# The second MLP matmul of a retention-and-MLP kernel: the plain product in every block in place of a seven-product form

## The chip, the cores and the metric

The kernel runs on one core of one Trainium2 chip. The metric is the time of one execution in microseconds (us). A "slow" or "fast" label stands beside each execution; slow means more than 1.5% above the fastest execution of the same kernel in the same rounds. The profile names the engines PE (TensorE matmul), PEld (TensorE weight load), DVE (VectorE), ACT (ScalarE), POOL (GpSimd) and SP.

## The reference

```python
def _attn_ref(q, k, v):                      # (8, 8, 576, 64) each
    scores = (1 / np.sqrt(64)) * q @ k.transpose(0, 1, 3, 2)
    ret = scores * Dmat                      # decay gamma ** (i - j), causal
    return ret @ v

def _moe_ref(x, w_in, w_out):                # x (4608, 512), w_in (512, 2048), w_out (2048, 512)
    h = x @ w_in
    g = h * np.cos(h)                        # the "gated units" of the middle layer
    return g @ w_out                         # the second MLP matmul
```

The kernel handles the 4608 tokens in nine blocks of 512. A block's second matmul multiplies 512 x 2048 gated units by 2048 x 512 second weights.

## The kernel before

Every operation is a task in a graph. A list scheduler in Python gives each task a planned length and fixes, once and for all, the order of instructions on every engine. Two forms of the second matmul exist. `plain2` is the ordinary product. `wino2` splits the units, the tokens and the output columns of a block in two and uses seven products in place of eight, at the price of sums of operands. The sums of second weights are made once (`wsums`), the sums of gated units in each block. The kernel before uses `plain2` for block 0 alone.

```python
class Kernel:
    PLAIN = (0,)
    ...
    def plain2(self, j, base, span):            # 4 token tiles x 16 units, 512 columns each
        for half in range(2):
            for tt in range(2):
                for qd in range(4):             # 16 tasks of 4 matmuls, planned at 864 ns
                    for f in range(4 * qd, 4 * qd + 4):
                        e.matmul(bank (128 x 512), gt[f] (128 tokens), w_out[f] (512 columns), ...)
                copy("act", bank -> os)         # 4 copies on ACT a block
            self.store(j, half, os)             # 512 KB
    ...
    def wino2(self, j, base, span):
        # 8 sums of gated units of 128 x 1024 on DVE: S1, S2, S3, S4, each in two parts
        # 7 products x 8 units x 2 token tiles = 112 matmuls of 256 columns, in three banks
        # 3 snapshots and 1 copy on ACT, 3 combinations of outputs on DVE
        ...
                if j == NTB - 1:                # the last block stores its last half in two parts
                    self.store(j, 1, os[1], (256, 512))
                    self.store(j, 1, os[1], (0, 256))
    ...
    def graph(self):
        ...
        for j in range(NTB):
            if j == 1:
                self.wsums()                    # 8 sums of second weights on DVE, two of them in place
            ...                                 # first matmul (mlp1) of block j + 1
            if j in self.PLAIN:
                self.plain2(j, base, PER)
            else:
                self.wino2(j, base + 900, 12200 if last else PER)
            ...                                 # attention sessions for blocks to come
```

(Shortened and partly paraphrased in comments; cuts are marked.) The scheduler also holds a model of how blocks of instructions reach TensorE, with the constant `FETCH = 6000` ns; two experiments use it.

## Time and profile before

| | before |
|---|---|
| time, median of first runs | 308.1 us (307.5 to 313.1) |
| profiled execution | 312.0 us, labelled slow, clock 0.994 |
| PE busy | 294.1 us, 95% of the span |
| DVE busy | 206.3 us, 66% |
| last matmul to end of span | 3.2 us |

"PE busy" is a union of modelled durations, so 95% is only a hint; the prediction below shows the lines from which it takes that PE sets the time. In the lines, `L763` is the first MLP matmul, `L886` the seven-product matmul, `L800` the plain second matmul, `L774` (DVE) makes the gated units `gt`, `L847` and `L853` make the sums `s` of gated units, and `L634`, `L643`, `L652`, `L661` are the small attention matmuls, which come in sessions of 128. `pt` (`L723`, DVE) holds the decayed scores, and `xt` is the attention output that ACT's copy (`L476`) hands to the first MLP matmul.

### The profile page before, as it was taken

To read this page: it belongs to the slowest core of one execution; us is meant where nothing else is said; L and a number is where in the kernel's file an instruction comes from. 1 tells how busy PE (TensorE), PEld (TensorE's weight loads), DVE (VectorE), ACT (ScalarE), POOL (GpSimd) and SP (SyncE) were. 2 spreads that over 40 slices of the span, in tenths; PEclk is the share of its full clock that TensorE was granted. 3 is DMA by queue.
4 is the path that set the end of the run, shared out by engine and by line. 5 is a ranking of instruction groups with operands and counts; after the bars stand their busy time and mean duration, and the time that the engine had idled before them with its cause. 6 is when DMAs were issued, how large, how long until landed. Compare 5 with 4: busy or idle time off the path is not lost.

```text
span 310.3 us, 10091 instructions
## 1 busy us (share of the span) xinstructions
PE 294.1 (95%) x4274; PEld 214.7 (69%) x4277; DVE 206.3 (66%) x371; ACT 188.3 (61%) x340; POOL 108.9 (35%) x134
## 2 busy tenths in 40 slices
PE   8987999799889999999998799999999999999995
PEld 8866755688778888567855375768656666666684
DVE  3574973475984769898478487775769667666641
ACT  3476843888959775856373566474686665455430
POOL 2261058759517581931362631312741000000000
PEclk9999999999999999999999799999999999999999
DMA  9999999999977999894999749269701100300123
GB/s 172 222 159 206 205 229 217 253 270 219 219 157 189 122 204 285 159 171 109 234 219 247 181 48 235 61 114 195 161 13 72 70 2 0 127 10 2 63 76 136
DMA packets 126397, 46.80 MB, mean 151 GB/s; under 512 B 105104, under 2 KB 122000, under 8 KB 126352
## 3 DMA queue, kind: packets, MB, share of 16 engines
q1 hardware_dynamic: 122128, 41.95, 63.3%
q0 software_dynamic: 4224, 4.19, 8.4%
q8 instruction: 34, 0.56, 0.8%
q14 instruction: 11, 0.09, 0.1%
HBM read 36.70 MB, written 9.44 MB: 149 GB/s over the span
## 4 chain that ended last, share of the span: by engine, by line
PE 87%; DVE 3%; ACT 3%; issue 2%; DMA 2%; POOL 2%; DVEq 0%
PE bk L763 39%; PE bk L886 32%; PE bk L800 4%; PE bk L418 2%; DMA stgq<-in_q_dram 2%; PE bk L661 2%; PE bk L652 2%; PE bk L634 2%; PE st L643 2%; PE bk L575 2%; DVE gt L774 1%; PE bk L593 1%; DVE pt L723 1%; POOL win L743 1%; POOL wout L747 1%
## 5 line engine op out<-in xcount | busy, mean ns | idle before, releaser
L774 DVE TENSOR_TENSOR gt<-bk,cb 128x256 bf16<-128x256 f32 (+1 forms) x192 | 103.7, 555 | 59.5 <-ACT cb L771 52.9
L763 PE MATMUL bk<-xt,win 128*128 128x256 bf16 (+1 forms) x768 | 140.1, 327 | 2.3 <-issue 1.3
L771 ACT ACTIVATE cb<-bk,cpi 128x256 bf16<-128x256 f32 (+1 forms) x192 | 108.4, 585 | 55.6 <-PE bk L763 54.0
L763 PEld LDWEIGHTS bk<-xt,win 128*128 128x128 bf16 x768 | 72.9, 98 | 44.0 <-issue 2.3
L512 POOL TENSOR_TENSOR natv<-stgv,wv 128x512 bf16<-128x512 f32 x38 | 41.3, 1097 | 36.1 <-DMA stgv<-in_v_dram 23.3
L477 POOL CAST natk<-stgk 128x512 bf16<-128x512 f32 x36 | 22.0, 626 | 62.0 <-DMA stgk<-in_k_dram 34.6
L557 POOL TENSOR_TENSOR qnat<-stgq,wq 128x512 bf16<-128x512 f32 x36 | 38.6, 1092 | 13.5 <-DMA stgq<-in_q_dram 5.9
L723 DVE TENSOR_TENSOR pt<-bk,tri 128x512 bf16<-128x512 f32 (+1 forms) x46 | 29.6, 683 | 14.8 <-PE st L643 12.8
L476 ACT ACTIVATE sbd<-st 128x512 bf16<-128x512 f32 x32 | 19.3, 603 | 22.6 <-PE st L643 22.4
L886 PE MATMUL bk<-wout,s 128*128 128x256 bf16 x256 | 32.2, 273 | 0.0
L886 PE MATMUL bk<-tw,s 128*128 128x256 bf16 x256 | 31.6, 273 | 0.5 <-DVE s L847 0.5
L886 PE MATMUL bk<-wout,gt 128*128 128x256 bf16 x256 | 31.6, 273 | 0.0
L886 PEld LDWEIGHTS bk<-wout,s 128*128 128x128 bf16 x256 | 24.7, 98 | 6.6
L886 PEld LDWEIGHTS bk<-tw,s 128*128 128x128 bf16 x256 | 24.6, 98 | 6.1 <-DVE s L847 0.8
L886 PEld LDWEIGHTS bk<-wout,gt 128*128 128x128 bf16 x256 | 24.7, 98 | 4.6 <-DVE pt L723 0.2
L476 ACT ACTIVATE sn<-bk 128x512 f32<-128x512 f32 x24 | 14.4, 604 | 18.7 <-PE bk L886 18.7
L476 ACT ACTIVATE xt<-bk 128x512 bf16<-128x512 f32 x36 | 23.1, 694 | 0.3 <-PE bk L661 0.2
L898 DVE TENSOR_TENSOR os<-bk,sn 128x512 f32<-128x512 f32 x24 | 16.4, 685 | 8.2 <-PE bk L886 8.2
L886 PE MATMUL bk<-tw,gt 128*128 128x256 bf16 x128 | 17.3, 282 | 0.0
L886 PEld LDWEIGHTS bk<-tw,gt 128*128 128x128 bf16 x128 | 12.9, 101 | 4.2 <-issue 0.6
L418 PE MATMUL bk<-one 128*128 128x128 bf16 x181 | 14.3, 244 | 1.1 <-DVE lq L441 1.1
L800 PE MATMUL bk<-wout,gt 128*128 128x512 bf16 x61 | 14.8, 379 | 0.2
(63 smaller groups left out, 230.7 us busy)
## 6 DMA issues: line engine op xcount, KB each, us to landing
stgk<-in_k_dram SPq DMA_DIRECT2D x32, 256.0 KB, 5.0
stgv<-in_v_dram SPq DMA_DIRECT2D x32, 256.0 KB, 5.4
out_dram<-os SPq DMA_DIRECT2D x15, 512.0 KB, 3.5
stgq<-in_q_dram SPq DMA_DIRECT2D x12, 512.0 KB, 7.0
stgq<-in_q_dram SPq DMA_DIRECT2D x8, 256.0 KB, 4.9
win<-in_moe_w_in_dram POOLq DMA_DIRECT2D x4, 512.0 KB, 7.6
wout<-in_moe_w_out_dram POOLq DMA_DIRECT2D x4, 512.0 KB, 14.7
out_dram<-os SPq DMA_DIRECT2D x6, 256.0 KB, 3.5
```

The costliest lines, as they stand in the source:

```text
L418: inst = e.matmul(ap(self.at(self.wb), 512, 0, 128, 0, [1, 128]), self.ONE.ap(), self.ONE.ap(), start=True, stop=True, skip_group_check=True)
L476: return self.one(eng, dur, lambda e: e.activation(dst(), src(), AF.Copy), r=r, w=w, **kw)
L477: return self.one(eng, dur, lambda e: e.tensor_copy(dst(), src()), r=r, w=w, port=True, **kw)
L512: self.one(ve, vd, lambda e, b2=b2: e.tensor_tensor(ap(self.at(t["natv"]), 1024, 0, 128, 512 * b2, [D, H], [1, D]), ap(self.at(t["stgv"]), ...
L557: self.one("dve" if fast else "pool", 620 if fast else 990, lambda e, t=t, y=y: e.tensor_tensor(ap(self.at(t["qnat"]), 1024, 0, 128, y * 5 ...
L723: self.one("dve", 610, lambda e, hp=hp: e.tensor_tensor(ap(self.at(pt), 1024, p0, n, 512 * hp, [64, 8], [1, 64]), ap(self.at(sc[hp]), 512, ...
L763: inst = e.matmul(ap(self.at(bk), 512, 0, 128, 0, [1, n]), ap(self.WIN, 4 * DFF, 0, 128, c * DFF + 128 * f, [1, 128]), ap(self.at(xt), 204 ...
L771: self.one("act", 70 + n, lambda e: e.activation(ap(self.at(cb), TB, 0, 128, 0, [1, n]), ap(self.at(bk), 512, 0, 128, 0, [1, n]), AF.Sin, ...
L774: self.one("dve", 75 + n / 0.96, lambda e: e.tensor_tensor(ap(self.at(gt), NF * TB, 0, 128, f * TB + 256 * h0, [1, n]), ap(self.at(bk), 51 ...
L800: inst = e.matmul(self.at(bk).ap(), ap(self.at(gt), NF * TB, 0, 128, f * TB + 256 * half + 128 * tt, [1, 128]), ap(self.WOUT, NF * DM, 0, ...
L886: inst = e.matmul(ap(self.at(bank), 512, 0, 128, 256 * tt, [1, 256]), l(f, tt), rr(f), start=(first and f == 0 and tt == 0), stop=True, sk ...
L898: self.one("dve", 610, lambda e: e.tensor_tensor(view(h, c), ap(self.at(bank), 512, 0, 128, 0, [256, 2], [1, 256]), ap(self.at(sn[name]), ...
```

## The change

The intent is to drop the sums, at the price of a seventh more multiplications in the second matmul (eight products for seven).

```diff
-    PLAIN = (0,)
+    PLAIN = tuple(range(NTB))
...
-            if j == 1:
+            if j == 1 and len(self.PLAIN) < NTB:
                 self.wsums()
```

## The prediction

> **What bounds the kernel now.** I read the page's first two parts first, then PE's own waits, then the table by stretches, then the chain in order of time, and last the groups by line with their shapes.
>
> The head of the page and PE's rows over 40 slices:
>
> ```profile
> PE 294.1 (95%) x4274; PEld 214.7 (69%) x4277; DVE 206.3 (66%) x371; ACT 188.3 (61%) x340; POOL 108.9 (35%) x134
> ...
> PE   8987999799889999999998799999999999999995
> ...
> DVE  3574973475984769898478487775769667666641
> ...
> PEclk9999999999999999999999799999999999999999
> ```
>
> PE is busy for 95% of the span, and DVE reaches nine tenths only in a few slices between about 50 and 150 us. So PE is the first suspect. "Busy" does not prove it, because a matmul's end is modelled. The table by stretches (us from the start) says where PE is not full:
>
> ```profile
> 24.00:55.00 31.00, 29.17 (x288) 19.74 (x282) 19.63 (x38) 18.67 (x40) 11.70 (x13) 1.00 1.21 214
> 55.00:80.00 25.00, 23.18 (x451) 19.64 (x452) 15.39 (x33) 21.32 (x45) 18.84 (x22) 1.00 1.11 245
> 80.00:100.00 20.00, 18.06 (x366) 15.08 (x364) 15.35 (x30) 15.11 (x33) 9.24 (x12) 1.00 0.85 184
> 100.00:125.00 25.00, 24.90 (x566) 21.42 (x565) 18.67 (x39) 18.12 (x41) 12.75 (x15) 1.00 1.03 198
> ...
> 150.00:175.00 25.00, 21.72 (x363) 14.05 (x361) 15.02 (x22) 13.01 (x21) 11.43 (x13) 0.97 1.04 233
> ```
>
> The columns are the stretch's length, then PE, PEld, DVE, ACT, POOL. From 24 to 100 us PE is idle for 1.83 + 1.82 + 1.94 = 5.6 us. After 100 us there is 0.1 us, one hole of 3.28 us, and then nothing: the later rows show 25.00 of 25.00. PE's waits name the causes:
>
> ```profile
> PE st L643 <- issue: 3.3, 1, 3.3
> PE bk L575 <- DVE gt L774: 1.0, 1, 1.0
> PE bk L886 <- DVE s L847: 0.5, 1, 0.5
> PE bk L575 <- DVE pt L723: 0.2, 1, 0.2
> PE bk L763 <- DVE gt L774: 0.2, 1, 0.2
> ```
>
> Each is one event. So from about 100 us the kernel is a queue of PE work with nothing in front of it, and the price of the change is the difference in PE work. The pitch of a matmul is read from the chain in order of time (start, length, what), where back-to-back matmuls stand as one piece:
>
> ```profile
> 43.22 3.45 PE bk L800 x16
> ...
> 126.15 8.63 PE bk L763 x40
> ...
> 293.95 13.12 PE bk L886 x120
> 307.09 0.60 ACT os L476
> ```
>
> L800 is the plain second matmul, already used for block 0 with 512 moving columns: 3.45/16 = 0.2156 us each. L763, the first matmul, has the same shape in later blocks: 8.63/40 = 0.2158. L886 is the seven-product form with 256 columns: 13.12/120 = 0.1093. The mean durations in the groups (379 and 273 ns) contain pipeline drain and are not pitches.
>
> **What the Trainium skill says.** (1) "TensorE: Matmul & The Clock Gate", section "Back-to-back issue gap", gives N/2.4 + 2.5 ns when warm: 109.2 ns for 256 columns and 215.8 ns for 512. The trace agrees (109.3 and 215.6 to 215.8). The same section also gives about 131 ns for 512 columns in a stream with weight loads; this trace contradicts that, and I use the trace. (2) Same page, section "Step-by-step: what each phase is for": the next weights load while a matmul runs. The trace agrees: a load of 98 ns stands before every 109 ns matmul without lengthening it. So the 48 loads fewer per block are worth nothing in themselves. (3) "SBUF — State Buffer", section "Who interferes with whom": a DVE instruction with two SBUF inputs contends with a GpSimd instruction that reads SBUF. The sums of gated units are such instructions, and the trace is consistent: most take 0.69 us, some up to 1.49 us, while POOL is at work. (4) "Runtime: NRT & Kernel Launch", section "Instruction fetch mechanics": instructions are fetched in blocks of 256. The trace has 34 packets of instructions, and PE's 8551 instructions make 33.4 blocks. The two "issue" holes (1.30 us at 28.5, 3.28 us at 169.5) could be late fetches; the profile does not show that they are.
>
> **The change part by part.** There are nine blocks of 512 tokens; block 0 is plain in both kernels, so eight change.
>
> PE, removed: 7 products x 8 units of 128 x 2 token tiles = 112 matmuls of 256 columns a block, 112 x 0.1093 = 12.24 us. Added: 4 token tiles x 16 units = 64 matmuls of 512 columns, 64 x 0.2156 = 13.80 us. The difference is 1.56 us a block and 8 x 1.56 = **12.5 us**. All of it is on the path: seven blocks mix it with first matmuls on a full PE, and the last block's second matmul is the pure tail (the piece of 120 above ends 0.02 us before the last copy).
>
> DVE, removed: the groups of all DVE lines give 12.5 + 12.4 + 11.8 + 11.8 = 48.5 us for the 64 sums of gated units, 16.4 us for the 24 combinations of outputs (L898), and 3.5 + 2.9 + 1.4 = 7.8 us for the sums of second weights (L826), which run at 35 to 55 us. That is 73 us, so DVE falls from 206 to about 134 us. Nearly all of it lies beside PE work. On the path are only the PE waits which a sum caused or delayed. In block 1, at 79 to 97 us, the chain goes through two long sums (0.89 and 0.68 us pieces around 83 to 85 us) and then the wait of 1.00 us for gt at 85.5, followed by 0.21 (pt), 0.55 (s) and 0.18 (gt): 1.94 us. Each wait also exposes a drain of about 379 - 216 = 163 ns, 0.65 us for four. At most **2.6 us** can come back; I take **2.0**, as some of the hole would be filled by another wait.
>
> ACT: three snapshots and one copy of 128x512 a block become four copies of 128x512; 4 x 0.60 us either way. Nothing.
>
> PSUM banks: a block's seven products hold three banks, the plain form holds one at a time. This can only help, and after 100 us PE has no wait to shorten. Small gaps of about 0.1 us (pieces of eight L886 that take 0.98 in place of 0.87) should thin out: **-0.3**.
>
> End: before, the last store is half of the second half's columns, issued as soon as the last copy ends at 307.69, and the span ends 2.6 us later. After, the last store is the whole 512 KB. The DMA issues show 3.5 us to landing as the median of both sizes, so I estimate **+0.6**, from the difference 3.5 - 2.6 with part of it doubted.
>
> The removed operations' instructions: 96 fewer on PE a block (768 in all, three blocks of 256). It makes late fetches less likely, not impossible. The profiled run took 312.0 us and is marked slow; the usual runs are 307.5 to 308.1. The 3.28 us hole and the lower clock after it nearly account for that, so the quick runs probably don't have the hole, and nothing is to be won from it.
>
> Sum: 308.1 + 12.5 - 2.0 - 0.3 + 0.6 = 318.9. I round down a little for a schedule with fewer constraints: **318.5 us**, 3.4% slower.
>
> **The rivals.** Rival A: DVE is the real bound of the middle stretches, and losing 73 us of it lets everything move up. For it: DVE reaches nine tenths at about 50 to 150 us, and POOL loses time to the shared port. Against: PE has almost no idle time after 100 us, which an engine waiting for DVE would have. Even if all 5.6 us of PE idle between 24 and 100 us and its drains (about 2 us) vanished, 308.1 + 12.5 - 7.6 + 0.6 = 313.6. This is the best case, just inside 2%.
>
> Rival B: the static order changes for the worse. The order of instructions is made from planned durations, and with other second-matmul tasks all engines are ordered anew; a session or load could land so that PE waits on it, or a fetch hole of about 3 us becomes part of every run. For it: the trace has two such holes. Against: the planned cost of the plain form (864 ns for four matmuls) is what the trace shows, and it holds fewer banks. It would make 321 to 324.
>
> Rival C: work on PE is hidden, as if the end were set by DMA. Against: DMA is at 0.07 to 0.15 of its time from 225 to 295 us while PE is full. It would leave 308; I give it almost nothing.
>
> **Range and chances.** The PE difference is well measured: the pitches are known within 0.3%, or 0.6 us over eight blocks. What is uncertain is the recovery (0 to 4 us), the new order (0 to 3 us worse) and the end (0 to 1). So 315.0 to 321.5 should hold it 8 times in 10. The bound for slower by over 2% is 314.3, which needs a recovery of 6.9 us or more against my 2.3: chance of within 2% 0.11, of faster 0.01, of slower 0.88.
>
> **What would show each step right or wrong.** Right: the L800 group has some 576 matmuls at a pitch of 0.216, and no L886; PE's idle after 100 us stays near zero apart from single holes; DVE falls to 134 us; PE idle in the stretch of 80 to 100 us shrinks by 1 to 2 us; the end from the last copy grows from 2.6 to about 3.2 us. Wrong: PE idle after 100 us that the kernel before didn't have (rival B), or PE idle between 24 and 100 us going to nearly none (rival A), or a pitch of the plain form below 0.21 us in a mixed stream. A mean clock below 0.99 in quick runs would also break the sum, since it assumes the same clock for both forms.

## The result, and the profile after

The changed kernel took 319.7 us (median of 4 executions, 319.2 to 320.4), against 307.8 us for the kernel before in the same runs. The ratio of the fast runs is 1.040, 95% interval 1.036 to 1.043. All ratios here are the mean time of one kernel's fast runs over that of the other's of the same rounds, so not quite the ratio of the quoted medians. The profiled execution (319.42 us) is fast, with a clock of 0.999. Its page begins:

```profile
PE 301.8 (95%) x3859; PEld 176.5 (56%) x3893; DVE 142.1 (45%) x275; ACT 188.9 (59%) x340; POOL 104.6 (33%) x134
...
PE   8978999899999999999999999899999999999995
...
DVE  3575830565636345286463444435534443434300
```

DVE lost a third of its work and PE is as full as before, over a longer span. The table by stretches (length, then PE, PEld, DVE, ACT, POOL):

```profile
80.00:100.00 20.00, 19.21 (x349) 13.76 (x351) 9.80 (x22) 16.27 (x37) 9.26 (x13) 1.00 0.88 181
100.00:125.00 25.00, 24.32 (x407) 16.13 (x408) 11.71 (x26) 15.88 (x36) 12.10 (x14) 1.00 0.95 193
...
225.00:250.00 25.00, 24.01 (x380) 12.21 (x383) 10.78 (x16) 16.07 (x28) 5.21 (x6) 1.00 0.12 44
```

At 80 to 100 us the idle time of PE fell from 1.94 to 0.79 us, but after 100 us PE is no longer full. Its waits name the idle time (total, times, longest):

```profile
PE bk L800 <- issue: 1.6, 10, 0.2
...
PE bk L661 <- issue: 1.2, 2, 0.6
...
PE bk L763 <- DVE gt L774: 0.6, 1, 0.6
```

The first line is no real idle time. The profile holds 542 of the 576 plain matmuls, and those ten gaps stand before pieces of three, seven or nineteen matmuls where four, eight or twenty were issued: the weight load is there and the record of the matmul is missing. The second line is real. It shows in the chain in order of time (start, length, what):

```profile
176.84 3.45 PE bk L800 x16
...
199.89 0.06 PE bk L661 x6
199.95 0.64 issue
200.59 0.40 PE bk L661 x25
...
228.51 0.57 issue
...
312.17 1.69 PE bk L800 x7
313.88 0.60 ACT os L476
```

A plain matmul in this mixed stream has a pitch of 3.45/16 = 0.2156 us, as in block 0. Two holes each cut a session of attention matmuls in two. The last copy ends at 314.48, so 3.2 us pass until the span ends at 317.7.

The profile of before that came first was of a slow execution, so a fast one was profiled later (run e1 below: 305.5 us span, clock 1.0). Against that one I made the accounts that follow. The matmul work of a trace is the number of matmuls by kind times their pitch (0.1093 us for 256 columns, 0.2156 to 0.2158 for 512, 0.056 and 0.042 for transposes, 0.0094 for an attention matmul of 64 x 64, which is 1.20 us for a session of 128). "Rest" is the time that passed less that work. It holds the start, idle time, exposed drains and slow clock. The counts come from the weight-load records, which are complete.

```
                 work    rest by 24.7   by 100    by last matmul   last matmul to end    span
before (e1)      277.0       9.4         21.2         25.2               3.2            305.5
changed          289.5       9.4         18.5         24.4               3.8            317.7
difference       +12.5       0.0         -2.7         -0.8              +0.6            +12.2
```

So of the 12.2 us, the matmul work is 12.5, the longer last store 0.6, and the rest gave 0.8 back: 2.7 us less waiting by 100 us, of which 1.9 us was lost again later.

### The profile page after: what moved, and what is told of

Read it like the earlier page. It is cut to its first block, busy times and chain, and to the rows that moved or that the text cites. A ratio compares the mean times of both kernels' runs of the same rounds, so it can differ in the third digit from the quotient of the medians.

```text
span 317.7 us, 9213 instructions
## 1 busy us (share of the span) xinstructions
PE 301.8 (95%) x3859; PEld 176.5 (56%) x3893; DVE 142.1 (45%) x275; ACT 188.9 (59%) x340; POOL 104.6 (33%) x134
## 4 chain that ended last, share of the span: by engine, by line
PE 90%; ACT 2%; issue 2%; DMA 2%; POOL 2%; DVE 1%; DVEq 0%
PE bk L763 39%; PE bk L800 38%; PE bk L418 2%; PE bk L661 2%; PE bk L575 2%; PE bk L652 2%; DMA stgq<-in_q_dram 2%; PE bk L634 2%; PE st L643 1%; POOL win L743 1%; POOL wout L747 1%; ACT cb L771 1%; PE bk L593 1%; ACT kt L476 1%; DVE pt L723 0%
## 5 line engine op out<-in xcount | busy, mean ns | idle before, releaser
L774 DVE TENSOR_TENSOR gt<-bk,cb 128x256 bf16<-128x256 f32 (+1 forms) x192 | 105.7, 558 | 112.1 <-ACT cb L771 106.7
L800 PE MATMUL bk<-wout,gt 128*128 128x512 bf16 x542 | 132.5, 379 | 3.0 <-issue 1.6
L800 PEld LDWEIGHTS bk<-wout,gt 128*128 128x128 bf16 x576 | 55.0, 98 | 59.7
L512 POOL TENSOR_TENSOR natv<-stgv,wv 128x512 bf16<-128x512 f32 x38 | 39.3, 1044 | 46.5 <-DMA stgv<-in_v_dram 27.4
L723 DVE TENSOR_TENSOR pt<-bk,tri 128x512 bf16<-128x512 f32 (+1 forms) x46 | 29.6, 683 | 36.8 <-PE st L643 24.5
L476 ACT ACTIVATE os<-bk 128x512 f32<-128x512 f32 x36 | 21.7, 603 | 25.3 <-PE bk L800 25.3
L476 ACT ACTIVATE kt<-bk 128x512 bf16<-128x512 bf16 x20 | 12.0, 607 | 6.1 <-PE bk L575 5.8
L418 PEld LDWEIGHTS bk<-one 128*128 128x128 bf16 x181 | 12.9, 112 | 1.2 <-DVE lq L441 1.1
L661 PE MATMUL bk<-pt,natv 64*64 64x64 bf16 x576 | 11.1, 194 | 1.6 <-issue 1.2
L634 PE MATMUL bk<-qt,kt 64*64 64x64 bf16 x512 | 9.9, 194 | 2.1 <-POOL natv L512 1.8
L643 PE MATMUL st<-natv,natk 64*64 64x64 bf16 x512 | 11.2, 195 | 0.0
L634 PEld LDWEIGHTS bk<-qt,kt 64*64 64x64 bf16 x512 | 7.8, 107 | 3.9 <-DVE gt L774 2.0
L661 PEld LDWEIGHTS bk<-pt,natv 64*64 64x64 bf16 x576 | 8.6, 106 | 2.2 <-issue 1.4
```

Of the source, the lines that this page charges most:

```text
L418: inst = e.matmul(ap(self.at(self.wb), 512, 0, 128, 0, [1, 128]), self.ONE.ap(), self.ONE.ap(), start=True, stop=True, skip_group_check=True)
L476: return self.one(eng, dur, lambda e: e.activation(dst(), src(), AF.Copy), r=r, w=w, **kw)
L512: self.one(ve, vd, lambda e, b2=b2: e.tensor_tensor(ap(self.at(t["natv"]), 1024, 0, 128, 512 * b2, [D, H], [1, D]), ap(self.at(t["stgv"]), ...
L634: yield lambda e, b2=b2, c=c: e.matmul(ap(self.at(sc[ph]), 512, 64 * s, 64, (4 * b2 + c) * 64, [1, 64]), ap(self.at(self.keys(u)["kt"]), 1 ...
L661: yield lambda e, b2=b2, c=c: e.matmul(ap(self.at(ob[u]), 512, 64 * hp, 64, (4 * b2 + c) * 64, [1, 64]), ap(self.at(self.keys(u)["natv"]), ...
L723: self.one("dve", 610, lambda e, hp=hp: e.tensor_tensor(ap(self.at(pt), 1024, p0, n, 512 * hp, [64, 8], [1, 64]), ap(self.at(sc[hp]), 512, ...
```

## The experiments

Theory: TensorE is the only bound, each changed block costs its 1.56 us of matmul work, and the release of VectorE gives 1 to 2 us back in block 1. Rivals: VectorE's release is worth much more and hides a larger cost; or the new static order, with its waits and late instructions, makes the difference. Later executions of the kernel before were often slower than its first ones: 21 of 33 took over 310 us. A ratio therefore has an interval of about a per cent, and I compare profiled executions through the account of work and rest as well. Each account is of one execution.

### e1: the kernel before once more

No edit.

> The kernel before, unchanged, for a profile in its fast state (the one given was of a slow execution with a 3.28 us hole on TensorE). If the hole belongs to the slow state, the profile shows TensorE idle after 100 us of under 0.5 us and a span near 305.8 us. If the hole is part of every execution, it is there again at about the same place, and the span is near 306 to 309 us.

Measured: 309.1 us median of 307.2 to 315.2, ratio 1.001 (0.990 to 1.013), which only says that it is the same kernel. The profiled execution took 307.19 us, span 305.5 us. The stretches that answer to those with a hole in the first profile:

```profile
80.00:100.00 20.00, 18.01 (x366) 15.03 (x364) 15.40 (x30) 15.04 (x33) 9.37 (x12) 1.00 0.88 187
...
150.00:175.00 25.00, 25.00 (x389) 16.39 (x387) 17.34 (x27) 16.08 (x26) 13.97 (x15) 1.00 1.07 234
```

PE is full from 150 to 175 us, and the span is near the expected 305.8, so the hole of 3.28 us is not part of every execution: of the two profiles of this kernel, the slow one has it and the fast one does not. It has a second price. These are two stretches of the slow execution, and the chain right after the hole:

```profile
169.50:172.80 3.30, 0.04 (x4) 0.05 (x8) 0.04 (x1) 0.00 (x0) 0.00 (x0) 1.00 1.12 326
173.50:176.90 3.40, 3.40 (x14) 1.81 (x12) 2.31 (x5) 2.74 (x6) 3.40 (x5) 0.50 0.72 148
```

```profile
172.97 0.25 PE bk L661 x30
173.22 1.55 PE bk L763 x4
```

The column before the DMA share is the granted clock: 0.50 for one window of 3.4 us after the hole. Four matmuls of 512 columns then take 1.55 us, 0.39 each in place of 0.216. In this window matmul work of 1.74 us (count times pitch) began in 3.41 us, so where PE is full it costs half of itself, 1.7 us. That is the most it costs: where PE would have waited anyway it is less, and the fastest executions of both kernels (306.07 and 319.24 us) have clocks of 0.994 and 0.995. Hole and window, 3.3 + 1.7 = 5.0 us, are about the 4.8 us between the two spans (310.3 and 305.5). The trace also holds each packet of the instruction queue (16,384 bytes). Beside the holes of PE in several runs, taken from the trace (us):

```
execution            packet on its way     hole of PE          landing to end of hole
before, slow          170.2 to 171.3     169.47 to 172.75              1.5
before, fast (e1)     166.0 to 167.1     none
changed               198.0 to 199.0     199.95 to 200.59              1.6
changed               225.8 to 227.7     228.51 to 229.08              1.4
e2                     88.2 to  89.4      89.19 to  90.92              1.5
e6                    102.0 to 103.3     103.37 to 104.83              1.5
e6                    169.4 to 170.9     170.40 to 172.42              1.5
```

Every one of these holes ends 1.4 to 1.6 us after a block of instructions has landed (1.3 to 1.6 us over the "issue" holes of over 0.4 us of all runs, the one at 28.6 us in e1 among them), and the fast execution, whose packet came some 4 us earlier, has none near 170 us. That they are late instruction blocks is therefore well supported. No run delays a packet alone.

### e2, e3, e4: two, five and eight blocks plain

```diff
-    PLAIN = (0,)
+    PLAIN = tuple(range(2))          # e3: range(5), e4: range(8)
-            if j == 1:
+            if j == len(self.PLAIN):   # the in-place sums of second weights wait for the last plain block
                 self.wsums()
```

> Blocks 0 and 1 plain, seven products from block 2 on. Theory (TensorE work counts, 1.56 us a block, and block 1 gives back 1 to 2 us of waits on VectorE): 306.9 to 308.1 us, so -0.2% to +0.2%. Rival (the new static order is what costs, in one lump at the first changed block): 309 us or more.

> Blocks 0 to 4 plain, seven products from block 5 on. Theory: 4 changed blocks x 1.56 = 6.2 less 1 to 2 given back in block 1: 311.7 to 312.7 us. Rival (a lump from the order or from late instruction fetches): not in line with the number of blocks, either under 310 or over 315 us.

> All blocks plain but the last, which keeps its seven products and its two small last stores. Theory: 7 x 1.56 = 10.9, less 1 to 2, no longer end: 316.4 to 317.4 us, 2 to 3 us under the changed kernel (1.56 of the last block and 0.6 of the longer last store). Rival (the last block is hidden or its cost is its end alone): within 1 us of the changed kernel.

Measured: e2 314.9 us (ratio 1.023, 1.015 to 1.030), e3 313.1 us (1.016, 1.010 to 1.023), e4 317.5 us (1.032, 1.024 to 1.040). In the account, with the time by which the last matmul ended:

```
           work     rest by 100   by 150   by last matmul    span
e1         277.0        21.2       22.6        25.2         305.5
e2         278.6        22.3       29.1        34.1         315.9
e3         283.2        19.1       20.6        24.9         311.4
e4         287.9        18.9       20.4        24.0         315.1
changed    289.5        18.5       20.2        24.4         317.7
```

Five, eight and nine plain blocks behave as the theory says: work grows by 1.56 us a block and rest stays at 24 to 25 us. (The times of e3 and e4 lie 0.4 and 0.1 us above their expected bands; e3's profile has two half-clock windows, before 63 us, for which the account is not corrected.) From e4 to the changed kernel the span grows by 2.6 us, of which the work is 1.6 and the end 0.6 (3.2 against 3.8). e2 is a clear miss of the theory and falls in the rival's range. It has less work than e3 and took longer: in its profile (the slowest of its six executions) it lost 6.8 us between 100 and 150 us, where the others lost 1.4 to 1.7. So something other than matmul work, here in one lump, can cost more than a block's matmuls.

### e9: two blocks plain, the sums of second weights early

The first suspect for e2 were the sums of second weights, which moved from 35 us into the busy stretch.

```diff
-            if j == len(self.PLAIN):
-                self.wsums()
+            if j in (1, 2):
+                self.wsums(j == 2)    # seven of the eight sums in block 1; one in-place sum in block 2
+        self.TW8 = sb("tw8", [128, 1024], BF16)   # the other in-place sum gets a tile of its own
-    ... s=9 ...
+    ... s=8 ...                       # room for it
```

> As the kernel with blocks 0 and 1 plain, but seven of the eight sums of second weights run in block 1 again, as in the kernel before (one of the two in-place sums has a tile of its own; one buffer fewer for the sums of gated units makes room). If the sums of second weights, moved into the busy stretch of 100 to 150 us, made that kernel slow: 309 to 311 us. If it is the first block of seven products itself, or the order: still 313 to 315 us.

Measured: 314.4 us, ratio 1.021 (1.016 to 1.027): the suspect falls. The profile's stretches:

```profile
80.00:100.00 20.00, 19.35 (x350) 13.89 (x353) 9.70 (x22) 16.22 (x37) 9.67 (x12) 1.00 0.80 172
100.00:125.00 25.00, 21.60 (x414) 16.21 (x412) 14.99 (x32) 15.95 (x35) 12.16 (x14) 1.00 0.97 190
```

At 80 to 100 us PE is as full as in the changed kernel, and at 100 to 125 us it idles for 3.40 us, in waits for `gt`, `pt`, `s` (DVE) and `xt` (ACT) of 0.3 to 0.8 us each. Its rest is 18.4 us by 100, 23.5 by 125, 25.2 by 150 and 30.0 at the end: from 100 to 150 us it lost 6.8 us, as e2 did. The loss stands where the first block of seven products starts. In e1 that is block 1, at 80 to 100 us; in e2 and e9 it is block 2. Why e3, whose first such block is block 5, pays nothing of the kind isn't settled by these runs.

### e8: seven products in block 0 too

```diff
-    PLAIN = (0,)
+    PLAIN = tuple(range(0))
-            if j == 1:
+            if j == len(self.PLAIN):
                 self.wsums()
```

> Seven products in block 0 too. Theory (TensorE work): 1.56 us less matmul work, but block 0 lies where TensorE already waits for others (5.6 us idle from 24 to 100 us), and the sums of the weights now stand before it: 306 to 310 us, most likely 308, no gain. Rival (only matmul work counts everywhere): 306.0 us.

Measured: 313.0 us (311.6 to 316.8), ratio 1.007 (0.996 to 1.017). The time lies above the expected 306 to 310 us, but the kernel before was slow in these rounds too (median 311.0), and no gain is what was expected. Work fell to 275.5, but rest grew to 31.2 (24.2 by 100 us): fewer matmuls, more waits.

### e5: the changed kernel with the sums of gated units put back, unused

```diff
     def plain2(self, j, base, span):
+        if j:
+            self.unused(j)     # the 8 sums S1 to S4 of wino2 on DVE; nobody reads them
```

> The changed kernel with the 64 sums of gated units put back on VectorE, their results unused; the result stays right. Theory (TensorE sets the time, VectorE's sums lie beside it): 319.7 to 321.5 us, the change from the sums being at most the 1 to 2 us they delay in the early blocks. Rival (VectorE's release was worth several us and hid part of a larger cost): 323 us or more.

Measured: 323.4 us (321.7 to 325.9), ratio 1.042 (1.032 to 1.052). By the time alone this is the rival's range (323 us or more). The ratio's interval overlaps that of the changed kernel, but e7 below, which is the changed kernel but for its last store, took 319.6 us in the same rounds, so the 3.8 us are likely real. In the account the work is the same 289.5 and the rest 28.4 in place of 24.4. Of these 4.0 us, 3.4 come after 125 us. The profile lists PE's waits:

```profile
PE bk L661 <- issue: 3.3, 3, 2.3
PE bk L763 <- issue: 1.9, 1, 1.9
```

Most of the growth is in holes before instructions (5.2 us in these two lines, 2.5 in the changed kernel), above all one of 2.34 us that ends at 175 us, 1.4 us after a block of instructions landed; the waits for `gt` are 1.1 us in place of 0.7. So the 45 us of extra work on VectorE (186.7 busy against 142.1) hardly made PE wait for it. The plan was made anew with the extra tasks; whether that or chance brought the long hole isn't shown, since the kernel before has such a hole in one of its two profiles.

The run says something on the 2.7 us that the change gave back, too. This is its stretch of 80 to 100 us:

```profile
80.00:100.00 20.00, 19.83 (x357) 14.26 (x356) 15.78 (x31) 16.45 (x36) 9.06 (x11) 1.00 0.91 180
```

VectorE is as busy as in the kernel before (15.40 us in e1), and yet PE idles for 0.17 us where e1 idles for 1.99; rest by 100 us is 18.9 us, against 18.5 in the changed kernel and 21.2 in e1. So the load on VectorE alone is not what held PE up in block 1. What is left is that matmuls no longer wait for sums, or the new order; no run parts these two.

### e6: seven products without any sums

```diff
-        for q in range(2): ...        # S1 to S4 removed
-            if j == 1:
-                self.wsums()
-            6: (left_s(2), right_t(2), ...),  5: (left_s(1), right_t(1), ...),  7: (left_s(3), ...), ...
+            6: (left_a(0, 1), right_b(0, 1), ...),  5: (left_a(1, 1), right_b(1, 1), ...),  7: (left_a(0, 0), ...), ...
```

> The kernel before with its seven products, but all sums of gated units and of second weights left out: the matmuls read gated units and second weights directly (wrong result on purpose, same matmuls in number and shape). Theory: 305.0 to 306.7 us, the waits on VectorE of block 1 being all that is gained. Rival (VectorE bounds the middle stretches): 303 us or less.

Measured: 313.9 us (311.9 to 315.2), ratio 1.011 (1.000 to 1.022), a miss of both. Taking the sums away did not speed the kernel up. PE's waits:

```profile
PE bk L763 <- ACT xt L476: 2.8, 2, 1.7
PE st L643 <- issue: 2.0, 1, 2.0
PE bk L661 <- issue: 1.5, 1, 1.5
```

Rest is 20.2 by 100 us, where e1 has 21.2, although it holds one half-clock window (59.8 to 63.2 us, at most 1.7 us) that e1 doesn't have. So 1.0 us came back by 100 us, and at most 2.7 with the window taken off. Then two late blocks (1.5 and 2.0), one wait for `xt` (1.7) and a second half-clock window (1.7) took 6.8 us, and rest ended at 31.6. As in the changed kernel, what comes back without the sums is early and small, and holes and waits elsewhere decide whether it is kept. Whether the new order brought them isn't shown; the hole of 2.0 us, at 170 us, stands where the slow execution of the kernel before has its own.

One thing that the sums did cost shows on POOL. Its product L512, in e1 and then in e6:

```profile
L512 POOL TENSOR_TENSOR natv<-stgv,wv 128x512 bf16<-128x512 f32 x38 | 41.2, 1096 | 34.8 <-DMA stgv<-in_v_dram 22.5 <-PE bk L661 12.2
```

```profile
L512 POOL TENSOR_TENSOR natv<-stgv,wv 128x512 bf16<-128x512 f32 x38 | 39.7, 1050 | 27.5 <-DMA stgv<-in_v_dram 16.5 <-PE bk L661 10.8
```

The same 38 instructions take 1096 ns each beside the sums and 1050 without (1044 in the changed kernel), as the port would make them that the Trainium skill calls shared ("SBUF — State Buffer", section "Who interferes with whom"). POOL isn't on the path, so this is worth nothing here.

### e12: the plain form with less matmul work

```diff
-        gt = self.gt[j]
+        gt, nf = self.gt[j], 14 if j else NF
-                        for f in range(4 * qd, 4 * qd + 4):
+                        for f in range(4 * qd, min(4 * qd + 4, nf)):
```

The planned length follows.

> The changed kernel with 14 of 16 units of the middle layer in the second matmul of blocks 1 to 8 (wrong result on purpose): 56 matmuls of 512 columns a block, 12.07 us, about the seven products' 12.24. Theory (matmul work is all that costs): 8 x 8 x 0.2156 = 13.8 us less than the changed kernel, 305.2 to 307.0 us. Rival (the plain form costs something beside its matmuls, banks or copies or order): 309 us or more.

Measured: 307.1 us (306.4 to 307.5), ratio 0.998 (0.993 to 1.003). It is the changed kernel less 64 of its 576 plain matmuls and 12.6 us faster, against 13.8 us of matmul work; the work of the account is 275.7, and the rest 26.3. By 100 us the rest is 17.9, less than the changed kernel's 18.5 in spite of a half-clock window at 26.2 us; later come a wait for `xt` of 1.55 us at 129 us and a hole of 0.93 at 173. The time lies a hair over the expected band and well under the rival's. With as much matmul work as the seven products have, the plain form is as fast as the kernel before. So no cost of the plain form beside its multiplications shows, within the half per cent of the interval.

### e7: the last store in two

```diff
-            self.store(j, half, os)
+                if j == NTB - 1 and half:     # one store of 256 KB per token tile, after its copy
+                    ... dma_start(out rows of tt, os columns of tt) ...
+            if j < NTB - 1 or half == 0:
+                self.store(j, half, os)
```

> The changed kernel with the last 512 KB store in two of 256 KB, one per token tile, each issued right after its copy. Theory: the end from the last copy to the end of the span falls from 3.2 to about 2.6 us, time 319.1 us. Rival (the end is latency of one transfer, whatever its size): no change, 319.7 us.

Measured: 319.6 us (318.9 to 321.4), ratio 1.030 (1.021 to 1.039), which can't be told from the changed kernel. In the profile the last copy ends at 314.77 and the span at 317.1, so 2.3 us in place of 3.2 in this one profile: the end did shrink, and its 0.9 us is below what the timing resolves.

### e10, e11: another plan, the same instructions

```diff
-    BACKLOG, FETCH, SLOW, MARGIN, SLACK, DX, DLAT = 3500, 6000, 3500, 60, 0, 1.18, 2400
+    BACKLOG, FETCH, SLOW, MARGIN, SLACK, DX, DLAT = 3500, 7500, 3500, 60, 0, 1.18, 2400
```

> The changed kernel, its order planned with 7.5 in place of 6.0 us for the coming of a block of instructions (the plan alone; no instruction is changed). If the holes of 0.64 and 0.57 us before attention matmuls at 200 and 228 us are late instruction blocks which the order can avoid: both gone, 318.0 to 318.8 us. Rival (the order does not matter to them, or a new order costs as much elsewhere): 319.2 us or more.

> The kernel before with the same change of its plan (7.5 in place of 6.0 us). If its slow executions come from a late block of instructions that the order can avoid: 306 to 308 us with no execution above 310. Rival: as many executions of 310 to 314 us as the kernel before has, or a new order that is slower throughout.

Measured: e10 (the changed kernel replanned) 324.2 us, ratio 1.053 (1.048 to 1.059); e11 (the kernel before replanned) 318.4 us, ratio 1.034 (1.029 to 1.039). Both hopes fall. Of e10's two holes after 100 us one is gone, but the other grew from 0.64 to 1.19 us, and that at 28 us from 1.32 to 2.57. e11's waits of PE:

```profile
PE bk L886 <- DVE s L847: 3.3, 3, 1.5
PE bk L661 <- issue: 2.4, 2, 2.1
PE bk L763 <- DVE pt L723: 2.1, 3, 1.7
```

Work differs from the parent's by 0.2 us in each, all warm-up matmuls before the real ones, but rest grew to 28.7 in e10 and 36.8 in e11. A new plan of the same instructions moved the kernel before by about 10 us and the changed one by 4.5 (e11's profile has two half-clock windows, at most 3.4 us of its 36.8). No run beats the kernel before with a right result.

## Why the prediction was right

The predicted time was 318.5 us in a range of 315.0 to 321.5, "slower" at 0.88; it measured 319.7. By its own steps:

**PE's matmul work, +12.5 us: right.** The plain pitch is 0.2156 us in the mixed stream too. From the last weight load of block 5's second matmul to that of block 8's, 67.2 us pass in e1 (234.7 to 301.9) and 71.9 us in the changed kernel (241.3 to 313.2): 4.7 us for three blocks, 1.57 each. e12 shows it from the other side, and e4 for the last block alone.

**Recovery of waits, -2.0 and -0.3: right in size by 100 us, too large at the end, and its reason only in part right.** By 100 us 2.7 us had come back. But 1.9 us were lost again after 100 us, so the term measured -0.8; most of what the forecast missed by is here. The reason was read from the slow profile, where block 1's wait of 1.00 us is for `gt` behind two sums. In the fast profile (e1) the same wait is put down to ACT's `xt`:

```profile
PE bk L575 <- ACT xt L476: 1.1, 1, 1.1
```

And e5 shows that PE stays full there with the sums back on VectorE, as long as nothing waits for them. That the size came out by 100 us is therefore partly luck. Of those 1.9, 1.21 are the two holes in attention sessions at 200 and 228 us, late instruction blocks by the table above; the other 0.7 is spread over gaps too small to name. The prediction expected fewer late blocks because PE has 768 instructions fewer. None of the changed kernel's four executions is labelled slow (they lie within 1.2 us), but four are few, and two short holes now stand in its fast execution, so the prediction's own sign for rival B showed in part.

**DVE to 134 us: off by 8.** It measured 142.1. The term added the busy times of the groups, which overlap: all groups of the kernel before add up to 214.4 us where the page says 206.3, those of the changed kernel to 143.8. That is 6 of the 8 us; the other 2 are the group of `gt`, which grew from 103.7 to 105.7. It did not matter, as DVE was off the path.

**ACT, nothing: right.** It went from 188.3 to 188.9. What the fewer banks gave by themselves no run shows.

**End, +0.6: right.** From the last copy to the end 2.6 us became 3.2 (e1: copy ends 302.87, span 305.5).

**Slow executions: right for the pair of profiles at hand.** e1's fast profile has no hole at 170 us, and hole and half-clock window account for the difference. The prediction also took a clock below 0.99 in quick runs as a sign against its sum. Two of the changed kernel's four executions have 0.989, and took 320.0 and 320.4 us where the other two took 319.2 and 319.4, so here it cost about a microsecond or less.

**Rival A (VectorE bounds the middle)** is refuted by e6 and e12, and by the full PE of e5's early stretch. **Rival B (order)** is no small matter: it did not decide this change, but e10 and e11, which change the plan alone, show that it is worth 4.5 to 10 us, and e2 and e9 lost 6.8 us in one lump. That the changed kernel got an order about as good as the tuned kernel before was partly luck, and the prediction's 0 to 3 us for it was too narrow a span. **Rival C** is refuted by the result itself.

## What to carry to other kernels

Where one engine is full for most of the span, price a change by the pitch of that engine's instructions from back-to-back pieces, not by their mean duration, and expect removed work on other engines to give back at most the waits that hang on its results. A static order is itself a large term: any edit that makes the planner reorder can add several us of new waits and late instructions, so judge a mechanism by an account of work and rest as well as by the time. Look for holes called "issue" and for halved-clock windows before comparing two executions.

## What the Trainium skill lacked or had wrong

- "TensorE: Matmul & The Clock Gate", section "Back-to-back issue gap": its figure of about 131 ns for 512 columns in a stream with weight loads isn't met here; the runs show 0.2156 to 0.2158 us, and the formula N/2.4 + 2.5 ns, which it gives for isolated matmuls, fits both widths of these streams (0.1093 us for 256).
- "Runtime: NRT & Kernel Launch", section "Instruction fetch mechanics": it calls the crossing of a 16 KiB boundary mostly hidden. Most are (3 of the changed kernel's 31 packets go with an "issue" hole of over 0.4 us), but by all signs above packets of 16,384 bytes came late in the middle of the kernel and left TensorE without work for 0.5 to 3.3 us, and work went on 1.3 to 1.6 us after the landing. The page has no figure for that lag.
- The first page again, Part 1, on the clock gate: it says the clock drops after an idle window of about 3.4 us. Half-clock windows of 3.4 us are here (0.50 after the hole of 3.28 us), but none of the twelve that begin inside a kernel in these traces followed a wholly idle one: the 3.41 us before each held 0.98 to 1.54 us of matmul work (count times pitch). The page's section on a second failure mode does name frequent short idles as a cause, without a figure. One followed a window in which PE was busy for 2.15 of 3.40 us, with small attention matmuls and transposes, while in e10 a stretch with 1.86 of 3.40 us busy (132.2 to 135.6) was followed by full clock, so busy time alone doesn't decide. These are two neighbouring stretches of e2:

```profile
56.00:59.40 3.40, 2.15 (x83) 1.78 (x75) 1.71 (x3) 3.10 (x7) 1.80 (x3) 1.00 1.19 258
59.40:62.80 3.40, 3.25 (x18) 2.39 (x19) 0.85 (x2) 1.52 (x5) 2.88 (x3) 0.50 0.81 177
```

- The same page says that the window runs free and that the slow matmuls at a kernel's start differ in number from run to run. It doesn't tell that half-clock windows in the middle of a kernel come and go between executions: clocks of 1.0, 0.994, 0.989 and 0.983 (none, one, two, three windows in 307 us, worked out as half of 3.4/307 a window) stand beside times of one kernel from 306 to 315 us, though not in step: the fastest has 0.994.
